# A new issue list for a state-space convolution and a linear attention that share one core

## The chip, the cores and the metric

The kernel runs on one core of one Trainium2 chip. The metric is the device time of one execution in microseconds (us), lower is better. Beside the plain times there is one profiled execution, in which the hardware profiler recorded each instruction of each engine.

## What is computed

Two independent heads read inputs of 2048 rows and 576 columns; their outputs stand side by side in one array of 2048 x 1152.

```python
def _A_ref(u, ...):                     # columns 0..575
    K  = 2.0 * einsum("dn,dnl->dl", C, P).real       # P = exp(A dt * position)
    Kf, Uf = rfft(K, 2 * L), rfft(u transposed, 2 * L)
    y  = irfft(Uf * Kf, 2 * L)[:, :, :L]
    return y transposed + u * D_skip
def _B_ref(x, wqkv, w_phi, wo):         # columns 576..1151, 32 heads of 18
    q, k, v = x @ wqkv
    phi_q, phi_k = softmax of +-(q w_phi), softmax of +-(k w_phi)
    kv, z = phi_k^T v, sum of phi_k
    o = (phi_q kv) / (phi_q z + 1e-6)
    return o @ wo
```

The first head is a long convolution done by Fourier transforms, the second a linear attention with a softmax feature map.

## The kernel before

The program first notes all its work as 2459 numbered operations and then issues them in the order of a written list. An operation is what one engine does in one go: a group of matmuls into one accumulation space (a "PE op"), one vector instruction, one transfer. There is no scheduler at run time: each engine takes its own operations in the order of the list, and an instruction that must wait holds up everything behind it on its engine. SP issues all 345 transfers.

- **Fold and gemms.** The weights are folded with w_phi and split into a high and a low part (wh, wl for the keys, vh, vl for the values). Each of 16 key tiles multiplies 128 rows of x with them (lines 410 to 428; in the rows `wh,x`, `wl,x`, `vh,x`, `vl,x`), splits x itself into two parts (`x<-zo,x`), takes the softmax (lines 430 to 468; its last multiply is `e<-e,small`), copies v, and adds to kv (`e,v`). Each of 16 query tiles does the same for q, transposes (`ident,e` at line 549), multiplies with kv (`kvb,fT`), transposes o (`ident,o`, lines 577 and 578), and multiplies with wo (`wh,x` and `wl,x` again, after the buffers changed hands).
- **Convolution.** 16 first transform stages of u (`ub,w`; the result is copied out of PSUM as `zi` and stored to DRAM), 18 groups that build the filter (`sel,mg` at PE, phases at line 757 on GpSimd, which the profile calls POOL, exponentials on ACT, products at lines 815 to 820 on VectorE, called DVE, and a sum by PE with `cs`), 4 first stages of the filter, 16 products (a turn `ub,ff`, the product itself on DVE and POOL, and a step back `cs,ff`; its factor ff is loaded at line 895, its part ub brought back from DRAM at line 904), and 16 last stages (`zi,w`, four stores each).

Everything that PE makes lies in one PSUM space of 8 banks. A bank can take the next accumulation only when DVE or ACT has copied the last one out (line 300 for a plain copy; lines 310 and 314 are two-operand instructions, of which some read PSUM). The buffers in SBUF turn over too: 2 of ff, zi and mg, 3 of e, ac, x, 5 of ub and cs, 7 of the small sums.

The list is the string ORDER from line 992. A word is an operation's number; an `x` behind it gives the operation to its other engine (DVE and POOL for SBUF work, ACT and DVE for copies out of PSUM), `@` gives the PSUM banks, and `:n` puts n filling matmuls ahead of a PE op. They multiply zeros into the space that the op will overwrite (line 237, rows `ident,zero`), and do nothing for the result; each takes PE's time and stands behind whatever the space has to wait for.

```python
if fill:
    ...
    for _ in range(fill):
        self.matmul(t[0:cols, 0:n], self.zero.t[0:rows, 0:cols], ...)
o[2](eng) if o[12] else o[2]()
...
for word in ORDER.split():
    word, _, fill = word.partition(":")
    word, _, at = word.partition("@")
    k = int(word.rstrip("x"))
    o = self.ops[k]
    ...
    self.emit(k, o, o[12][0] if word[-1] == "x" else o[0], int(fill or 0), at)
```

Before, the list holds 118 filling matmuls at 13 places: 49 at the start of the program, 11 ahead of the third first stage of u, 58 elsewhere.

## Time and profile before

| | |
|---|---|
| median of 3 runs | 544.55 us (543.78 to 545.48) |
| the profiled execution's own time | 545.11 us |
| its span, first to last instruction | 543.3 us |
| mean granted TensorE clock | 0.998 |
| busy: PE, DVE, ACT, POOL | 521.5, 455.9, 382.1, 328.8 us |
| DMA | 107.01 MB, 197 GB/s over the span |

The profile's times start with the span. "Busy" of PE counts matmuls by modelled ends, which overlap a little. A row `psum<-ub,w 64*128 64x288 f32 x8` reads: eight matmuls into PSUM from the weights ub (or w) and the moving tile, in a tile of the array of 64 rows by 128 columns, each on 64 partitions x 288 elements. What stands in brackets is the idle time before the row's first instruction and what ended it. For the reading below the span is cut in three: 0 to 213 us (the key tiles, the first stages of u, the first groups), 213 to 397.6 us (most of the groups, the query tiles' beginning), 397.6 us to the end (products, last stages, the other query tiles).

### The profile page before, as it was taken

Reading aid. Unit: us, or ns where it says so; the run is one execution under the profiler, and the core shown is the slowest. Engines: PE = TensorE matmul, PEld = TensorE weight load, DVE = VectorE, ACT = ScalarE, POOL = GpSimd, SP = SyncE. Lnnn points to the kernel's source line nnn. Section 1 sums busy time; section 2 is a strip of 40 time slices with the busy share of each in tenths; the row PEclk is TensorE's granted clock in tenths of the full one; section 3 lists DMA queues with packets and bytes.
Section 4 is the critical chain, followed back from the end, with each engine's and each line's share of the span. In section 5 each row is a group of like instructions: output and inputs, shape, how many; then the busy total and the mean of one; then the engine's idle time right before and its main releaser. Section 6 shows DMA issues by size and latency. Waiting matters only on the chain.

```text
span 543.3 us, 19242 instructions
## 1 busy us (share of the span) xinstructions
PE 521.5 (96%) x8192; PEld 435.9 (80%) x8192; DVE 455.9 (84%) x716; ACT 382.1 (70%) x555; POOL 328.8 (61%) x456
## 2 busy tenths in 40 slices
PE   8999999999999989999999999999899999999995
PEld 7999899888888767888878666766689877776984
DVE  7999899898868889999989996999974889787641
ACT  4868798798559799889689977989733444343332
POOL 1173885958777775982758998997433617434300
PEclk9999999999999999999999999999999999999999
DMA  8936711244245678246664588756458789998785
GB/s 235 326 105 195 281 45 31 101 139 134 89 139 190 207 241 294 83 128 196 229 205 118 153 265 250 241 180 194 131 173 271 234 281 293 287 281 260 265 252 157
DMA packets 86163, 107.01 MB, mean 197 GB/s; under 512 B 5698, under 2 KB 70338, under 8 KB 86078
## 3 DMA queue, kind: packets, MB, share of 16 engines
q1 hardware_dynamic: 86078, 105.79, 61.5%
q8 instruction: 64, 1.05, 0.8%
q14 instruction: 21, 0.17, 0.1%
HBM read 61.22 MB, written 44.54 MB: 195 GB/s over the span
## 4 chain that ended last, share of the span: by engine, by line
PE 69%; DVE 13%; DMA 7%; ACT 4%; issue 3%; SPq 2%; POOL 1%; DVEq 0%; ACTq 0%; POOLq 0%
PE psum L295 63%; PE psum L549 3%; DMA ff<-in_ff_dram 2%; DMA dram<-zi 2%; PE psum L237 2%; DVE ac L314 1%; DVE cs L816 1%; SPq L979 1%; PE psum L577 1%; DMA cs<-dram 1%; DVE e L310 1%; DMA ub<-dram 1%; DVE e L314 1%; DVE small L434 1%; DVE small L437 1%
## 5 line engine op out<-in xcount | busy, mean ns | idle before, releaser
L295 PE MATMUL psum<-vh,x 128*128 128x288 f32 x576 | 123.6, 301 | 0.5 <-ACT ks L300 0.5
L295 PE MATMUL psum<-wh,x 128*128 128x288 f32 x576 | 124.1, 302 | 0.0
L757 POOL TENSOR_TENSOR cs<-cs,pi 128x32 int32<-128x32 int32 (+4 forms) x180 | 108.5, 608 | 8.0
L295 PEld LDWEIGHTS psum<-wh,x 128*128 128x128 f32 x576 | 94.1, 188 | 7.7 <-issue 4.2
L295 PEld LDWEIGHTS psum<-vh,x 128*128 128x128 f32 x576 | 94.0, 188 | 5.4 <-issue 3.2
L295 PE MATMUL psum<-vl,x 128*128 128x288 f32 x320 | 93.8, 295 | 0.0
L295 PE MATMUL psum<-wl,x 128*128 128x288 f32 x320 | 93.7, 295 | 0.0
L811 ACT ACTIVATE psum<-psum 128x512 f32<-128x512 f32 x108 | 59.9, 588 | 15.4 <-PE psum L295 14.9
L295 PEld LDWEIGHTS psum<-vl,x 128*128 128x128 f32 x320 | 60.2, 188 | 0.0
L295 PEld LDWEIGHTS psum<-wl,x 128*128 128x128 f32 x320 | 60.2, 188 | 0.0
L310 POOL TENSOR_TENSOR x<-zo,x 64x128 fp32r<-64x128 f32 (+1 forms) x30 | 25.4, 848 | 46.3 <-ACT x L394 35.1
L310 POOL TENSOR_TENSOR e<-e,small 128x1152 f32<-128x1152 f32 (+1 forms) x24 | 41.2, 1720 | 14.5 <-DVE small L450 7.8
L815 DVE TENSOR_TENSOR cs<-psum,cs 128x1024 f32<-128x1024 f32 x36 | 43.6, 1212 | 3.7 <-ACT psum L811 3.6
L310 POOL TENSOR_TENSOR e<-small,e 128x576 f32<-128x576 f32 x26 | 30.6, 1177 | 25.4 <-DVE small L437 23.6
L816 DVE TENSOR_TENSOR cs<-psum,cs 128x1024 f32<-128x1024 f32 x36 | 43.6, 1214 | 1.4 <-PE psum L295 1.3
L295 PE MATMUL psum<-ub,ff 64*32 64x288 f32 x1024 | 40.0, 410 | 4.3 <-DMA ff<-in_ff_dram 1.9
L295 PEld LDWEIGHTS psum<-kvb,fT 126*128 126x128 f32 (+1 forms) x320 | 38.3, 188 | 7.2 <-issue 2.9
L295 PEld LDWEIGHTS psum<-cs 128*32 128x32 f32 x2304 | 34.1, 110 | 11.2 <-issue 2.9
L295 PE MATMUL psum<-cs 128*32 128x64 f32 x2304 | 40.0, 220 | 2.6 <-DVE cs L816 0.9
L295 PE MATMUL psum<-kvb,fT 126*128 126x133 f32 (+1 forms) x320 | 41.6, 280 | 0.1
L440 ACT ACTIVATE e<-e 128x1152 f32<-128x1152 f32 x32 | 37.0, 1164 | 2.7 <-POOL e L310 1.3
L781 ACT ACTIVATE cs<-cs 128x1040 f32<-128x1040 int32 x36 | 38.3, 1064 | 0.6 <-POOL cs L776 0.4
(156 smaller groups left out, 1115.2 us busy)
## 6 DMA issues: line engine op xcount, KB each, us to landing
dram<-zi SPq DMA_DIRECT2D x32, 576.0 KB
ub<-dram SPq DMA_DIRECT2D x64, 288.0 KB
dram<-zo SPq DMA_DIRECT2D x32, 288.0 KB
zo<-in_xT_dram SPq DMA_DIRECT2D x24, 320.0 KB
zi<-dram SPq DMA_DIRECT2D x12, 576.0 KB
ub<-in_u_dram SPq DMA_DIRECT2D x16, 288.0 KB
xd<-x SPq DMA_DIRECT2D x8, 576.0 KB
x<-xd SPq DMA_DIRECT2D x8, 576.0 KB
```

Of the source, the lines that this page charges most:

```text
L237: self.matmul(t[0:cols, 0:n], self.zero.t[0:rows, 0:cols], self.data.t[0:rows].bitcast(BF16)[:, 0:n], start=not o[13], stop=not o[13], ski ...
L295: pe.matmul(o, l, r, start=start, stop=stop, skip_group_check=skip)
L310: op(eng, [c_dve(n[0]) if e == "dve" else c_pool(n[1]) for e in eng], lambda e: (dve if e == "dve" else pool).tensor_tensor(dst(), a(), b( ...
L314: op(eng, c_dve(n) if eng == "dve" else c_pool(n), lambda: e.tensor_tensor(dst(), a(), b(), op=alu), r=r, w=w, with_=with_, lock=eng == "p ...
L434: op("dve", c_dve(D), lambda: dve.tensor_reduce(two(top.t), v(), axis=AX.X, op=ALU.max, negate=True), r=[p], w=[top])
L440: op("act", c_act(1152) + 40, lambda: act.activation(e.t, e.t, AF.Exp), r=[e], w=[e], table="exp")
L549: pe.transpose(tp.t[0:m, j - j0, :], e.t[:, sign, 7 * g:7 * g + GRP[g], :].rearrange("p h f -> p (h f)"), ident.t)
L757: op("pool", c_pool(2 * n * W), lambda n=n, j=j: pool.tensor_tensor(x()[:, :, :, n:2 * n], x()[:, :, :, 0:n], pi.t[:, j:j + 2, gs].bitcast ...
L781: act.activation(cs.t[:, 1], cs.t[:, 1].bitcast(I32), AF.Sin, scale=TURN)
L811: op("act", c_act(512), lambda b=b: act.activation(b.t, b.t, AF.Exp), r=[b], w=[b], table="exp")
L815: op("dve", c_dve(64 * W), lambda: dve.tensor_tensor(F(), both(M.t), F(), op=ALU.mult), r=[M, cs], w=[cs])
L816: op("dve", c_dve(64 * W), lambda: dve.tensor_tensor(E.t[:, :, :, 32:64], both(up.t), cs.t[:, :, :, 0:32], op=ALU.mult), r=[up, cs], w=[E])
```

## The change

Only the string ORDER differs: the same 2459 operations with the same tiles, buffers and costs, in another order. The list was made by small moves in which transfers are taken late and delays are random. Its first lines stand for the whole:

```diff
 ORDER = """
-0 1 2 3 1097 1093 4 68 1094 5 1096 1154 1104 1105 1107 1092 1108 1109 51 34 1095 6 27 7@0:49 20 1106 1110 1111 1112 1113 1114 1115 8 35@2 1199 1137 11
-28@4 29 52 12 1116 1120 9 53x 30 36 10 54 13 22@6 32 37 21 1117 39 992 1118 1119 40 15@0 14 1074 23 31 33 1121 38 1063 1003 344 18 25 16 345 24
...
+1093 32 12 22 1116 1154 39 15@0 1117 52 1096 30 38 23 1192 992 344 1094 41 25 1137 14 53 40 54 33 18 31 26 1004@42:2 1118 1076 360 16 24 1119 345 19
+1074 68 346x 1121 17 347 42 1080 1122 1075 1127 287 1123 57@6 56 1161 43 1125 288 348@0 1124 1126 1077 44 1128 1079 1006 1129 1130 349 47 289x 1131 45
...
```

The whole string counts 481 PE ops in both versions. Of the operations, 133 change their engine and 319 their banks; an operation moves by 7 places in the list in the median, by 14 in the mean, and some by hundreds. Filling matmuls: 151 at 43 places in place of 118 at 13; 49 still stand at the start, 2 in place of 11 ahead of the third first stage of u, and 100 in place of 58 elsewhere (2 to 3 at most places).

The first place is on PE, in the first stretch, where the seventh group starts (the trace has it at 188 to 193 us before). `cs` and `e,v` are earlier work, `ub,w` first stages of u, `sel,mg` three parts of the group, `fT,e` transposes of kv. Before:

```order
L295 MATMUL psum<-cs 32x64 x32
L295 MATMUL psum<-e,v_2823 19x36 x32
L295 MATMUL psum<-ub,w_225 128x288 x4
L295 MATMUL psum<-sel,mg 128x512 x2
L295 MATMUL psum<-ub,w_225 128x288 x4
L295 MATMUL psum<-sel,mg 128x512 x2
L295 MATMUL psum<-fT,e 128x126 x5
```

and the changed list, at the same group:

```order
L295 MATMUL psum<-cs 32x64 x32
L295 MATMUL psum<-e,v_2773 19x36 x32
L295 MATMUL psum<-ub,w_219 128x288 x4
L237 LDWEIGHTS zero
L237 MATMUL psum<-ident,zero 128x256
L237 LDWEIGHTS zero
L237 MATMUL psum<-ident,zero 128x256
L295 MATMUL psum<-sel,mg 128x512 x2
L295 MATMUL psum<-ub,w_219 128x288 x4
L237 LDWEIGHTS zero
L237 MATMUL psum<-ident,zero 128x256
```

Two filling matmuls now stand ahead of the group's first part, and four ahead of its second (the first of them is the last row); the neighbours are the same.

The second place is on DVE and POOL, in the key tiles' softmax. `e<-e,small` of 1152 elements is its last multiply, `x<-zo,x` the split of x, `cs<-ac,cs` work of the filter's parameters. Before, on DVE:

```order
L442 TENSOR_REDUCE small<-e 128x2x32 x2
L450 RECIPROCAL small<-small 128x64
L310 TENSOR_TENSOR e<-e,small 128x1152
L310 TENSOR_TENSOR x_552<-zo,x_552 128x512
L310 TENSOR_TENSOR e<-small,e 128x576
L314 TENSOR_TENSOR cs<-ac,cs 128x640
L450 RECIPROCAL small<-small 128x64
L310 TENSOR_TENSOR e<-e,small 128x1152
```

and in the changed list, on POOL (`cs<-cs,pi` is the phases of the filter):

```order
L487 MEMSET v_685 128x32
L752 MEMSET cs 128x16
L310 TENSOR_TENSOR e<-e,small 128x1152
L753 COPY cs<-pi 128x16x2
L757 TENSOR_TENSOR cs<-cs,pi 128x16x2
L757 TENSOR_TENSOR cs<-cs,pi 128x16x2x4
L310 TENSOR_TENSOR x_623<-zo,x_623 64x128
L310 TENSOR_TENSOR e<-e,small 128x1152
```

Of the 16 such multiplies DVE had 4 and POOL 12; now DVE has 1 and POOL 15. Of the 24 splits `x<-zo,x` of 128x512 DVE had 13 and now has 11; POOL does the rest.

The third place is on PE, in the last stretch, at a product's step back (`cs,ff`, which reads the factor ff that a transfer brings). `kvb,fT` is a query tile's product, `ident,o` its transposes. Before:

```order
L295 MATMUL psum<-ub,ff 32x288 x32
L295 MATMUL psum<-kvb,fT 128x133 x8
L295 MATMUL psum<-kvb,fT 128x76 x2
L295 MATMUL psum<-cs,ff 64x288 x16
L577 MATMUL psum<-ident,o 128x128 x4
L578 MATMUL psum<-ident,o 128x128
```

and the changed list:

```order
L295 MATMUL psum<-kvb,fT 128x133 x6
L237 LDWEIGHTS zero
L237 MATMUL psum<-ident,zero 128x256
L237 LDWEIGHTS zero
L237 MATMUL psum<-ident,zero 128x256
L295 MATMUL psum<-kvb,fT 128x133 x2
L295 MATMUL psum<-kvb,fT 128x76 x2
L295 MATMUL psum<-cs,ff 64x288 x16
L237 LDWEIGHTS zero
L237 MATMUL psum<-ident,zero 128x256
L295 MATMUL psum<-vh,x_7078 128x288
```

Here filling matmuls stand inside the query tile's product and behind the step back, and a gemm follows in place of the transposes.

## The prediction

> **What bounds the kernel now.** First the page: the span and the busy shares.

> ```profile
> span 543.3 us, 19242 instructions
> PE 521.5 (96%) x8192; PEld 435.9 (80%) x8192; DVE 455.9 (84%) x716; ACT 382.1 (70%) x555; POOL 328.8 (61%) x456
> ```

> PE is busy for 96% of the span. So a new order can gain at most what PE idles, and it loses whatever it adds to PE's own work. The second view is the table by stretches (columns: stretch, length, busy PE, PEld, DVE, ACT, POOL with counts, granted clock, DMA share, GB/s).

> ```profile
> 0.00:213.00 213.00, 206.42 (x3246) 184.72 (x3246) 185.89 (x283) 168.24 (x226) 137.43 (x220) 1.00 0.52 169
> 213.00:397.60 184.60, 177.93 (x3137) 138.31 (x3137) 174.17 (x273) 158.29 (x236) 141.66 (x197) 1.00 0.59 182
> 397.60:538.30 140.70, 137.12 (x1817) 112.83 (x1809) 95.89 (x163) 54.88 (x92) 49.67 (x40) 1.00 0.83 260
> 538.30:543.30 5.00, 0.00 (x0) 0.00 (x0) 0.00 (x0) 0.65 (x1) 0.00 (x0) 0.82 0.52 171
> ```

> PE idles 213.00 - 206.42 = 6.58 us in the first stretch, 6.67 in the second, 3.58 in the third, and the 5.00 behind its last matmul, where only the last stores run. The clock is 1.00 in all three, so none of this is throttling. DVE is the engine next to the bound: 174.17 of 184.60, 94%, in the middle; DMA is at 0.83 in the last stretch. The third view is PE's list of waits in each stretch (what was waited for, us in total, times, longest): first stretch, middle, last.

> ```profile
> PE psum L295 <- ACT zi L300: 1.7, 2, 1.2
> PE psum L237 <- DVE zero L333: 1.6, 1, 1.6
> PE psum L295 <- DVE zi L300: 0.6, 1, 0.6
> PE psum L295 <- POOL v L487: 0.6, 1, 0.6
> ```

> ```profile
> PE psum L295 <- DMA ub<-dram: 1.5, 2, 1.2
> PE psum L549 <- DVE ac L314: 1.0, 1, 1.0
> PE psum L295 <- DVE cs L816: 0.9, 1, 0.9
> PE psum L295 <- DVE e L314: 0.8, 1, 0.8
> ```

> ```profile
> PE psum L295 <- DMA ff<-in_ff_dram: 1.9, 3, 0.9
> ```

> One wait, 1.6 us for the zeros at the very start, can't be moved by this list. The rest is many small waits, mostly for a PSUM bank that DVE or ACT has yet to copy out, and in the last stretch for the factor ff of a product.

> **The change, part by part.** The sum is made against the profiled execution, 545.11 us (span 543.3 and 1.8 around it), which lies 0.56 above the median of 544.55. Only the order, some engines and the filling matmuls change.

> *Filling matmuls, the sure part.* The timeline of PE around the third first stage of u, and where the eighth group's filler stands before (start, length of the row, line, operation, in brackets the idle time ahead of it; the rows of DVE are the two instructions that hold PE there):

> ```profile
> 14.60 1.26 PE L237 MATMUL psum<-ident,zero 64*128 64x256 bf16 x10
> 15.60 0.51 PE L295 MATMUL psum<-ub,w 64*128 64x288 f32 x1
> ```

> ```profile
> 189.61 1.24 PE L295 MATMUL psum<-ub,w 64*128 64x288 f32 x8 [0.63 <-DVE zi L300]
> 192.03 0.49 PE L295 MATMUL psum<-sel,mg 64*128 64x512 f32 x2 [1.18 <-ACT zi L300]
> ```

> ```profile
> 213.12 0.50 PE L295 MATMUL psum<-sel,mg 64*128 64x512 f32 x2 [0.80 <-DVE e L314]
> 213.79 1.03 PE L237 MATMUL psum<-ident,zero 64*128 64x256 bf16 x8 [0.16 <-DVE zi L300]
> 214.66 1.19 PE L295 MATMUL psum<-ub,w 64*128 64x288 f32 x7
> ```

> Ten fillers from 14.60 to 15.60 are 0.10 us each, and no wait stands at either end: the 9 of 11 that go save 9 x 0.10 = **0.9** (from nothing, if the operands of what follows come late, to 1.0).

> *Filling matmuls, the open part.* 42 more stand elsewhere: 42 x 0.10 = 4.2 us of PE's time. A filler costs nothing where PE would have stood still while it ran. But the rows at 213.79 say that it needn't: it writes the bank that its op will write, waited 0.16 for that bank to be copied out, and then eight of them ran 0.87 (214.66 - 213.79) ahead of the real work. What waits for a bank pays them in full; what waits for an operand (the case of the group's parts, whose selected rows or transposes come late) hides them. The row at 192.03 is the case in which two fillers, 0.2, would be paid or hidden whole: 1.18 of idle time stood there. Bounds 0 and +4.2; I take the middle, **+2.1**, because neither kind is the rule in the waits above.

> *Work moved from DVE to POOL.* The groups of instructions by form (count, busy us and mean ns):

> ```profile
> L310 DVE TENSOR_TENSOR e<-e,small 128x1152 f32<-128x1152 f32 x4 | 5.7, 1426 | 0.1
> L310 DVE TENSOR_TENSOR x<-zo,x 128x512 fp32r<-128x512 f32 x13 | 10.0, 772 | 0.2 <-ACT x L394 0.2
> ```

> ```profile
> L310 POOL TENSOR_TENSOR e<-e,small 128x1152 f32<-128x1152 f32 x12 | 27.3, 2272 | 7.9 <-DVE small L450 7.8
> L310 POOL TENSOR_TENSOR x<-zo,x 128x512 fp32r<-128x512 f32 x11 | 14.2, 1291 | 18.3 <-ACT x L394 18.1
> ```

> Three softmax multiplies and two splits leave DVE: 3 x 1.426 + 2 x 0.772 = 5.8 us less of 185.89 in the first stretch; POOL gains 3 x 2.272 + 2 x 1.291 = 9.4 over 137.43. DVE falls from 87% to 85% there, POOL rises from 65% to 69%, so copies out of PSUM come sooner. The idle time that this and the new order can reach is 6.58 - 1.6 = 5.0. The two waits for `zi` come to 1.7 + 0.6 = 2.3, and the rows at 189.61 and 192.03 put 0.63 and 1.18 of it at the first place shown above, behind copies that a less loaded DVE (and an ACT that takes fewer of them) ends sooner. I take **-2.3**, with 0 and -5.0 as bounds. If POOL is late instead, the cover is gone: see the fourth rival.

> What is left on DVE may get dearer. This row is a split on DVE early in the program, while POOL was hardly at work:

> ```profile
> 11.16 0.69 DVE L310 TENSOR_TENSOR x<-zo,x 128x512 fp32r<-128x512 f32 x1
> ```

> 0.69 against the mean of 0.772 over 13, a tenth more where POOL works beside it. [...]

> *Broken pairs of PE ops.* Counted in the two lists, a gemm follows a gemm directly 4 times less, and a turn `ub,ff` another turn 6 times less. The timeline:

> ```profile
> 448.47 0.30 PE L295 MATMUL psum<-wl,x 128*128 128x288 f32 x1
> 448.61 0.43 PE L295 MATMUL psum<-wh,x 128*128 128x288 f32 x2
> ...
> 450.07 0.29 PE L295 MATMUL psum<-wl,x 128*128 128x288 f32 x1
> 450.29 0.96 PE L295 MATMUL psum<-ub,ff 64*32 64x288 f32 x24
> ```

> ```profile
> 477.33 0.72 PE L295 MATMUL psum<-zi,w 64*32 64x288 f32 x16
> 478.99 2.18 PE L295 MATMUL psum<-ub,ff 64*32 64x288 f32 x64 [0.94 <-DMA ff<-in_ff_dram]
> 481.10 0.40 PE L295 MATMUL psum<-wh,x 128*128 128x288 f32 x1
> 481.34 0.29 PE L295 MATMUL psum<-wl,x 128*128 128x288 f32 x1
> 481.47 0.43 PE L295 MATMUL psum<-wh,x 128*128 128x288 f32 x2
> ```

> Within a gemm the next matmul starts 0.14 later (448.47 to 448.61), into a turn 0.22 (450.07 to 450.29): 0.08 more. Coming back, the first step of a gemm takes 0.24 (481.10 to 481.34) against 0.13 for the next: 0.11 more. So 4 gemms x 0.19 + 6 turns x 0.08 = **+1.2**, between 0.3 and 1.9 (all ten at 0.19). [...]

> *The waits for ff.* Three of them, 1.9 in all, 0.94 at 478.99. Such a transfer lasts longer than the gap it has to fit into, as the chain of what ended last shows (start, length):

> ```profile
> 474.50 4.36 DMA ff<-in_ff_dram
> 486.86 4.95 DMA ff<-in_ff_dram
> ```

> The buffer of ff comes free with an earlier product's step back, and the next transfer runs from there. At the third place shown above and at three more products the changed list puts 0.3 to 0.8 us more of PE's work between the two. I take **-1.2** of the 1.9, bounds 0 and -1.9; late-taken transfers behind other transfers of SP could make it +1.

> *Bank and operand waits in the middle.* The group at 213.12 (0.80 idle) gets its eviction 2.8 us of PE's work earlier, and the 1.0 at line 549 goes in the new neighbourhood: -1.8. Seven PE ops newly stand close behind the copy that they need; I price each with the 0.16 of the row at 213.79, +1.1. Sum **-0.7**, between -2 and +3 (one 0.8 wait at half of the seven), since DVE at 94% in this stretch does no work less.

> The tail behind PE's last matmul, 5.00, has the same operations in nearly the same order: 0.

> Sum: -0.9 + 2.1 - 2.3 + 1.2 - 1.2 - 0.7 = **-1.8**; 545.11 - 1.8 = 543.3 for an execution like the profiled one, 542.75, so **542.8**, on the scale of the median.

> **The rivals.** What can be told apart from no change here is about 0.3%, 1.6 us.

> *The fillers are paid, no wait goes.* The middle stretch keeps its DVE at 94%, banks come as late as now, and fillers behind a bank wait are paid in full as at 213.79. -0.9 + 4.2 + 1.2 = +4.5: 549.1. It decides as soon as more than 13 of the 42 are exposed while all waits stay (13 x 0.10 + 0.3 = 1.6). For it: the row at 213.79. Against it: 5.0 us of idle time lie in a stretch where DVE is relieved.

> *The waits go, and the fillers eat it.* -0.9 - 2.3 + 4.2 + 1.2 - 1.2 - 0.7 = +0.3: 544.9, no change.

> *All goes well.* The first stretch's 5.0 go wholly and the fillers stand only where PE would wait: -0.9 - 5.0 + 0 + 1.2 - 1.2 - 0.7 = -6.6, 538.0. Against it: the waits are many and small, and a list that moves all neighbours seldom takes them all away without new ones.

> *POOL becomes late.* A softmax multiply takes 2.272 on POOL and 1.426 on DVE: the kv product of that key tile gets its operand 0.85 later, behind phases that POOL has queued ahead of it (second place above), and those phases feed the groups. Three such waits are 2.5, and the relief fails: -1.8 + 2.3 + 2.5 = +3.0, 547.6. Against it: with twelve such multiplies on POOL the first stretch shows one wait for POOL, 0.6.

> **How the numbers follow.** The forecast gets 0.40, and its own range is 540.5 to 545.0: 0.30 of it lie more than 1.6 us below the median, 0.10 within. The second rival (544.9) gets 0.15, the third (538.0) 0.12, the first (549.1) 0.18, the fourth (547.6) 0.15. Faster by over 0.3%: 0.30 + 0.12 = 0.42; within: 0.10 + 0.15 = 0.25; slower: 0.18 + 0.15 = 0.33. For the range I leave out what lies below the third rival and above the first by more than half of one of the smaller terms: 538.0 to 549.5.

> **What would show it.** In the profile of the changed kernel: the row of fillers ahead of the third first stage of u has 2 in place of 10, and the stages behind it come 0.9 sooner; the rows `ident,zero` elsewhere carry bracketed idle time, or stand where none would be (paid); PE's idle time in the first stretch falls from 6.6 towards 4.3, with DVE's busy time there about 180; the group at 213 has no wait for DVE's `e`; the waits for ff come to about 0.7. PE's busy time should be 1 to 4 us more. Wrong would be: first-stretch idle time as before or waits on POOL's `e` (the fourth rival), or busy time up by over 4 with idle time as before (the first).

## The result

The changed kernel is slower: 550.57 us in the median of 4 runs (549.37 to 551.48) against 544.16 of the kernel before (542.90 to 545.48), a ratio of 1.0116 with a 95% interval of 1.0084 to 1.0148. In a second measurement, on the chip of the run after_again below, it was 1.0155 (1.0129 to 1.0181). Forecast were 542.8, with a range from 538.0 to 549.5.

The page of the changed kernel, the span and the busy times:

```profile
span 548.7 us, 19305 instructions
PE 525.4 (96%) x8225; PEld 439.6 (80%) x8225; DVE 453.8 (83%) x711; ACT 374.3 (68%) x550; POOL 344.0 (63%) x465
```

The table by stretches, with the last two borders moved by the 5.4 us that the span is longer (columns as in the prediction):

```profile
0.00:213.00 213.00, 205.98 (x3255) 186.09 (x3255) 179.26 (x277) 164.07 (x225) 150.92 (x227) 0.99 0.53 172
213.00:397.60 184.60, 177.16 (x3053) 137.29 (x3051) 172.96 (x267) 155.62 (x233) 140.44 (x197) 0.99 0.57 180
397.60:543.70 146.10, 141.68 (x1922) 115.93 (x1920) 101.62 (x169) 53.95 (x92) 52.60 (x41) 0.99 0.79 248
```

PE is busy for 3.9 us more and idle for 1.5 more. The granted clock, in the column behind the counts, is 0.99 in each stretch, where it was 1.00. And PE's waits have other names. The lists below are cut a little later, at 220 and 403 us, to hold the same work: first stretch, middle, last.

```profile
PE psum L295 <- DVE wl L367: 2.3, 1, 2.3
PE psum L295 <- issue: 1.9, 3, 1.0
...
PE psum L237 <- ACT zi L300: 1.2, 1, 1.2
PE psum L295 <- ACT zi L300: 0.5, 2, 0.3
```

```profile
PE psum L237 <- DVE ac L314: 1.0, 2, 0.9
PE psum L295 <- DVE cs L815: 1.0, 2, 0.6
PE psum L577 <- ACT zo L608: 0.9, 1, 0.9
```

```profile
PE psum L295 <- DMA cs<-dram: 2.0, 1, 2.0
PE psum L577 <- DVE o L314: 1.1, 1, 1.1
PE psum L295 <- ACT zo L300: 0.4, 1, 0.4
PE psum L295 <- DMA ff<-in_ff_dram: 0.4, 1, 0.4
```

Some old waits shrank as forecast (ff 1.9 to 0.4, the parts of a group behind `zi` from 1.18 to 0.3 at most), and others came, two of them about 2 us long, longer than any that the kernel before had behind its start. (`issue` is idle time for which the profile shows no releaser; it was 0.3 in the first stretch before.)

To see where the time goes, one can compare how far both are with the same work. I gave each PE op its usual price, summed the prices in the order of each list, and compared the times at which the sums reach the same value. (The prices are the 20th percentile of the intervals of that kind of op in both traces. Another choice of prices moves single entries by up to about 1 us; the last entry is read from the two traces alone.)

```
time before     20.2  61.9  144.2  198.5  209.2  234.4  287.2  376.8  423.0  529.9  last matmul
changed - before -1.6  -2.6   -2.4   -2.9   +0.2   +1.2   +0.7   +2.3   +3.6   +2.6   +6.5
```

So the first 198 us win 2.9, the next 36 lose 4.1, the 295 us behind that lose 1.4, and the last 8 us lose 3.9. Behind the last matmul 4.5 us of stores follow, 5.6 before.

The largest loss has one place. PE around it (start, length, idle time in brackets):

```profile
199.89 0.29 PE L295 MATMUL psum<-wl,x 128*128 128x288 f32 x1
202.45 2.29 PE L295 MATMUL psum<-ub,w 64*128 64x288 f32 x8 [2.26 <-DVE wl L367]
204.67 0.61 PE L295 MATMUL psum<-wh,x 128*128 128x288 f32 x1
205.07 0.44 PE L295 MATMUL psum<-wl,x 128*128 128x288 f32 x1
...
205.84 0.43 PE L295 MATMUL psum<-wh,x 128*128 128x288 f32 x2
```

and the same place microsecond by microsecond, in the columns of the table by stretches:

```profile
201.00:202.00 1.00, 0.00 (x0) 0.00 (x0) 0.36 (x3) 1.00 (x4) 1.00 (x2) 1.00 0.98 390
202.00:203.00 1.00, 0.55 (x2) 0.50 (x4) 0.50 (x3) 1.00 (x2) 1.00 (x1) 0.58 1.05 429
203.00:204.00 1.00, 1.00 (x6) 0.68 (x4) 0.00 (x0) 1.00 (x2) 0.31 (x2) 0.50 0.95 389
204.00:205.00 1.00, 1.00 (x5) 0.34 (x2) 0.22 (x1) 1.00 (x2) 1.00 (x1) 0.50 0.92 207
205.00:206.00 1.00, 1.00 (x7) 1.00 (x7) 1.00 (x2) 1.00 (x2) 0.94 (x1) 0.71 0.97 343
```

PE stands still for 2.26 us, and just as it goes on, its clock is granted at 0.50, for 3.41 us (202.17 to 205.58). The first stage of u, 1.24 long elsewhere, takes 2.29. The trace has two more such stretches of 3.41 us before the last matmul, at 215.82 and at 536.67, each behind waits (1.23 and 2.02). They count as busy PE: that is where part of the 3.9 us comes from.

### The profile page after: what moved, and what is told of

The parts are those of the page before. It is cut to its first block, busy times and chain, and to the rows that moved or that the text cites. A ratio compares the mean times of both kernels' runs of the same rounds, so it can differ in the third digit from the quotient of the medians.

```text
span 548.7 us, 19305 instructions
## 1 busy us (share of the span) xinstructions
PE 525.4 (96%) x8225; PEld 439.6 (80%) x8225; DVE 453.8 (83%) x711; ACT 374.3 (68%) x550; POOL 344.0 (63%) x465
## 4 chain that ended last, share of the span: by engine, by line
PE 70%; DVE 11%; ACT 8%; issue 4%; DMA 3%; POOL 3%; SPq 0%; DVEq 0%; ACTq 0%; POOLq 0%
PE psum L295 64%; PE psum L549 2%; PE psum L237 2%; DVE ac L314 1%; ACT psum L811 1%; DMA cs<-dram 1%; PE psum L577 1%; DVE cs L815 1%; POOL e L310 1%; ACT cs L785 1%; DVE cs L816 1%; DMA x<-xd 1%; DMA ff<-in_ff_dram 1%; ACT L811 1%; ACT zi L300 1%
## 5 line engine op out<-in xcount | busy, mean ns | idle before, releaser
L295 PE MATMUL psum<-vh,x 128*128 128x288 f32 x576 | 125.0, 304 | 0.3 <-DVE e L314 0.2
L295 PE MATMUL psum<-wh,x 128*128 128x288 f32 x576 | 124.1, 302 | 0.8 <-issue 0.6
L757 POOL TENSOR_TENSOR cs<-cs,pi 128x512 int32<-128x512 int32 (+4 forms) x180 | 107.1, 607 | 5.4
L295 PEld LDWEIGHTS psum<-wh,x 128*128 128x128 f32 x576 | 94.6, 189 | 8.2 <-issue 4.6
L295 PEld LDWEIGHTS psum<-vh,x 128*128 128x128 f32 x576 | 95.4, 191 | 6.6 <-issue 3.7
L295 PE MATMUL psum<-vl,x 128*128 128x288 f32 x320 | 94.5, 297 | 0.0
L295 PE MATMUL psum<-wl,x 128*128 128x288 f32 x320 | 93.9, 295 | 0.0
L310 POOL TENSOR_TENSOR e<-e,small 128x1152 f32<-128x1152 f32 (+1 forms) x30 | 50.5, 1688 | 21.1 <-DVE small L314 14.9
L295 PEld LDWEIGHTS psum<-vl,x 128*128 128x128 f32 x320 | 61.0, 191 | 0.0
L295 PEld LDWEIGHTS psum<-wl,x 128*128 128x128 f32 x320 | 60.6, 189 | 0.0
L310 POOL TENSOR_TENSOR x<-zo,x 64x128 fp32r<-64x128 f32 (+1 forms) x29 | 25.7, 885 | 35.7 <-ACT x L394 26.6
L310 POOL TENSOR_TENSOR e<-small,e 128x576 f32<-128x576 f32 x26 | 31.0, 1195 | 22.9 <-DVE small L437 21.3
L816 DVE TENSOR_TENSOR cs<-psum,cs 128x1024 f32<-128x1024 f32 x36 | 43.7, 1214 | 0.4 <-PE psum L295 0.2
L295 PE MATMUL psum<-ub,ff 64*32 64x288 f32 x1024 | 41.5, 410 | 1.7 <-ACT zo L300 0.4
L295 PEld LDWEIGHTS psum<-kvb,fT 126*128 126x128 f32 (+1 forms) x320 | 38.4, 189 | 5.2 <-issue 0.9
L295 PE MATMUL psum<-kvb,fT 126*128 126x133 f32 (+1 forms) x320 | 41.2, 278 | 0.4 <-DVE cs L815 0.4
L295 PE MATMUL psum<-cs 128*32 128x64 f32 x2304 | 40.6, 221 | 0.8 <-DVE cs L820 0.6
L295 PEld LDWEIGHTS psum<-cs 128*32 128x32 f32 x2304 | 34.9, 110 | 8.0 <-issue 3.4
```

The lines of the kernel that those rows point to most:

```text
L295: pe.matmul(o, l, r, start=start, stop=stop, skip_group_check=skip)
L310: op(eng, [c_dve(n[0]) if e == "dve" else c_pool(n[1]) for e in eng], lambda e: (dve if e == "dve" else pool).tensor_tensor(dst(), a(), b( ...
L757: op("pool", c_pool(2 * n * W), lambda n=n, j=j: pool.tensor_tensor(x()[:, :, :, n:2 * n], x()[:, :, :, 0:n], pi.t[:, j:j + 2, gs].bitcast ...
L816: op("dve", c_dve(64 * W), lambda: dve.tensor_tensor(E.t[:, :, :, 32:64], both(up.t), cs.t[:, :, :, 0:32], op=ALU.mult), r=[up, cs], w=[E])
```

## The experiments

The first reading was that of a late load (theory L). The load for the first stage at 202.45 is issued at 194.50 in the changed list and 129.69 in the old one, and `wl` at line 367 seemed done long before. The wait of 2.0 for cs near the end has a load as late. Rivals: fillers are the cost (F), the stall alone counts and the clock does not follow it (W), SP's stores set the end (S). Four kernels were run on one chip. All ratios below are to the kernel before, run beside them on the same chip; the changed kernel itself gave 1.0116 in one such measurement and 1.0155 in another, so ratios from two such measurements compare only to about 0.004, 2 us.

```diff
 changed list: load of u, first stage 0
-... 1034@26 387 394 ... 415 993 ...
+... 1034@26 993 387 394 ... 415 ...
```

> The changed list, with one word moved: the load of u for first stage 0 is issued some 11 us sooner, before two weight loads. Theory L (late loads and the clock): in the changed kernel this load is issued at 194.50 and PE, ready for it at 200.19, starts at 202.45; 2.3 us of standing still, and from 202.16 to 205.57 the granted clock is 0.50, which costs about 1.2 more. So the wait at 200 goes, the clock there stays at 1.00, and the time falls by 2.5 to 4, to a ratio of 1.004 to 1.007 to the kernel before. Rival F (the 42 added filling matmuls are what was paid): the wait is used up by the next bank wait, time falls by under 1, ratio 1.010 or more. Rival W (the stall alone counts, the clock does not follow it): -2.0 at most, and the clock is low somewhere else.

```diff
 changed list: load of cs, last stage 11
-... 2410 2457 2458 ... 2424 2437 ...
+... 2410 2424 2457 2458 ... 2437 ...
```

> The changed list, with one word moved: the load of cs for last stage 11 is issued behind that of last stage 9, some 6 us sooner, ahead of eight output stores. Theory L: in the changed kernel PE waits 2.02 for it at 534.2, and the granted clock is 0.50 from 536.7 to 540.0, about 1.4 more; so time falls by 2 to 3.5, ratio 1.005 to 1.008. Rival S (SP's issue of stores at about 0.63 each sets the end, not PE): PE ends sooner but the time falls by under 1, ratio 1.010 or more, since the stores behind the load are as many as before. Rival F: under 1 as well.

Both moves together:

> The changed list with both words moved. Theory L: the two add up, -5 to -7 us, the ratio to the kernel before is 0.998 to 1.003 and nothing else of the change costs much on balance. Rival F: -1 to -3, ratio 1.006 to 1.010. Rival S: as the first of the two alone, -3, ratio 1.005.

```diff
 changed list: fillers ahead of the two PE ops
-... 994@24 ... 2425@2 ...
+... 994@24:20 ... 2425@2:18 ...
```

> The changed list with both loads as late as they are, and filling matmuls ahead of the two PE ops that wait for them: 20 ahead of first stage 0 of u and 18 ahead of last stage 11. They need a free bank, not the load, so by theory L they run while PE would stand still: waits as long as before, but PE looks busy, the clock stays at 1.00 behind them, and the time falls by 1.5 to 2.6, ratio 1.006 to 1.010. If low clock has nothing to do with the stall (rival W): no change or +0.5 to +1, ratio 1.011 to 1.014, with the clock low at the same places.

Measured, in this order: 1.0124 (1.0090 to 1.0159), 1.0134 (1.0098 to 1.0171), 1.0150 (1.0116 to 1.0183) and 1.0227 (1.0188 to 1.0265). Theory L fell. With the load 11 us sooner, PE of u0_early waits as before:

```profile
203.64 1.47 PE L295 MATMUL psum<-ub,w 64*128 64x288 f32 x8 [2.27 <-DVE wl L367]
```

In fill_cover the fillers themselves waited 2.26 for `wl`, since it is the bank that isn't free, and then ran in front of the real work; the clock fell all the same: over the first 213 us it is 0.98 in the mean, 0.99 in the other three. The 38 cost 4 to 5 us against the other three (557.80 against 552.37 to 553.79). That is the danger that the prediction saw in the row at 213.79. In l11_early PE's wait for cs is gone, and its last matmul comes at 543.9 where u0_early's comes at 544.5; yet the two spans, 550.6 and 550.5, are the same. SP issues 20 stores in a row there, with two more behind them before the end:

```profile
532.93 13.38 SPq L979 DMA_DIRECT2D out_dram<-ot  x20
```

That is 0.67 each, and the row ends at 546.3, behind the last matmul. So for the end rival S fits: this wait of PE was not on the path alone. (Rival F forecast the same time; the row of stores speaks for S.) The trace of both_early shows the link. There the wait for cs is gone too, and PE waits as long at the next gemm, for a copy by ACT that itself waits for a store to free its buffer:

```profile
535.10 0.40 PE L295 MATMUL psum<-vh,x 128*128 128x288 f32 x1 [2.03 <-ACT ot L300]
534.40 0.65 ACT L300 ACTIVATE ot<-psum 128x576 f32<-128x576 f32 x1 [6.60 <-DMA out_dram<-ot]
```

The name in the bracket at 202.45 was right, then, and one has to follow it. DVE and ACT of the changed kernel ahead of 202:

```profile
198.24 0.28 DVE L300 COPY e<-psum 36x133 f32<-36x133 f32 x1
201.64 0.25 DVE L300 COPY e<-psum 36x95 f32<-36x95 f32 x1 [3.12 <-ACT e L300]
201.81 0.58 DVE L367 TENSOR_TENSOR wl<-psum,wh 128x72 fp32r<-128x72 f32 x2
```

```profile
196.06 1.28 ACT L781 ACT_TABLE_LOAD   x1
197.35 1.07 ACT L781 ACTIVATE cs<-cs 128x1040 f32<-128x1040 int32 x1
198.33 1.15 ACT L785 ACTIVATE cs<-cs,hp 128x1040 f32<-128x1040 f32 x1
199.38 1.06 ACT L781 ACTIVATE cs<-cs 128x1040 f32<-128x1040 int32 x1
200.34 1.15 ACT L785 ACTIVATE cs<-cs,hp 128x1040 f32<-128x1040 f32 x1
201.39 0.38 ACT L300 ACTIVATE e<-psum 36x76 f32<-36x76 f32 x2
```

Two short copies into the buffer e stand on ACT behind a table load and four waves, 5.3 us of work. A DVE copy into the same buffer waits 3.12 for the first of them. Behind it on DVE stand the two small `wl` instructions, and only they free the bank of the first stage of u (theory Q). The remedy is two letters:

```diff
 changed list: two kv copies, ACT to DVE
-... 374 ... 369 ...
+... 374x ... 369x ...
```

The next four ran on one chip. head_new and tail_old are sewn from both lists: the first words of one, then all operations not yet issued in the order of the other.

> The changed kernel once more, unchanged, as the base for the other runs on this chip. All theories: 1.008 to 1.016 against the kernel before.

> The changed list with two words given to the other engine: two copies of the kv sums out of PSUM (76 columns of 36 rows each) go from ACT to DVE. In the changed kernel they stand on ACT behind a table load and four waves; a DVE copy into the same buffer waits 3.12 for the first of them at 201.64, with the two wl instructions behind it that free the bank of first stage 0 of u. Theory Q (a queue on a queue: PE's wait at 200 is this DVE wait, which is this ACT queue; the low clock follows the wait): the wait of 2.3 goes, so does the 3.4 us of half clock behind it, and the time falls by 2.5 to 4, 0.005 to 0.007 below the run of the changed kernel beside it. Rival F (the added filling matmuls are the cost): under 1 us, ratio within 0.002 of it.

> A list sewn of both: the first 806 words of the changed list (to about 185 us), then all other operations in the order and with the banks, engines and fillers of the list before. In the traces PE of the changed kernel is 2.5 to 2.9 us ahead at 170 to 198 us (the same base work done) and 6.5 behind at its last matmul. Theory Q, and with it that the loss lies behind this point: faster than the kernel before by 1 to 3 us, ratio 0.994 to 0.998. Rival F, or a cost that the changed list's first part hands on (buffers, POOL late): 1.000 to 1.006.

> A list sewn of both: the first 2339 words of the changed list (to about 510 us), then the rest as in the list before. At that place PE of the changed kernel is 2.5 us behind, at the end 6.5; behind its last matmul come 4.5 us of stores, 5.6 in the kernel before. Theory T (the last stretch of the list costs some 2 to 4 by itself, by the late load of cs with its half clock and by SP's stores): 0.004 to 0.007 below the changed kernel beside it, at about 1.005 to the kernel before. Rival: the tail only hands on what comes late, the ratio stays within 0.002 of the changed kernel's.

Measured: after_again 1.0155 (1.0129 to 1.0181), copies_dve 1.0071 (1.0041 to 1.0100), head_new 0.9937 (0.9921 to 0.9952), tail_old 1.0148 (1.0129 to 1.0166). Theory Q held: the two letters take 0.0084, 4.6 us, and the intervals don't meet. PE of copies_dve at this place:

```profile
200.45 0.29 PE L295 MATMUL psum<-wl,x 128*128 128x288 f32 x1
200.67 1.24 PE L295 MATMUL psum<-ub,w 64*128 64x288 f32 x8
201.84 0.40 PE L295 MATMUL psum<-wh,x 128*128 128x288 f32 x1
...
202.60 0.43 PE L295 MATMUL psum<-wh,x 128*128 128x288 f32 x2
```

No wait, and no half clock before its last matmul. From the first stage's start to the fourth row it takes 1.93 here (200.67 to 202.60) and 3.39 in the changed kernel (202.45 to 205.84): 1.5 us is what the half clock cost there, beside 2.26 of waiting. The rest lies near the second stretch at half clock, which copies_dve, at 0.999 over its span, doesn't have; in its place it has a wait of 1.02 for DVE's `e` at 223. Over the whole span PE is busy for 4.3 us less, with as many instructions and fillers:

```profile
PE 521.1 (96%) x8225; PEld 436.7 (80%) x8225; DVE 454.2 (83%) x713; ACT 373.6 (69%) x548; POOL 344.5 (63%) x465
```

So three stretches at half clock come to 4.3 us, an estimated 1.4 each.

head_new shows the other side: the changed list's first 806 words, to about 185 us, are a gain that lasts, 0.0063 or 3.4 us. This sewn list beats both kernels (541.33 us against 545.00). Theory T fell with tail_old: with the old list's last 120 words the loss is the same, and PE still waits for cs:

```profile
PE psum L295 <- DMA cs<-dram: 1.4, 1, 1.4
```

Left over are the fillers and the second half. The four kernels of the next chip:

```diff
 copies_nofill: copies_dve without its fillers behind the third first stage of u
-... 1482@72:2 ... 2057@4:3 ...
+... 1482@72 ... 2057@4 ...
 second_new: the first 1304 words of the list before, then the changed list
 second_nofill: second_new without the 63 fillers behind the seam
 before_u2: the list before
-... 1004@42:11 ...
+... 1004@42:2 ...
```

> The changed list with the two kv copies on DVE, and without its 100 filling matmuls beside the 49 at the start and the 2 at the third first stage of u. With them, that list took 1.0071 of the kernel before. Theory F (fillers are paid, 0.10 us each): up to 10 us less, ratio 0.990 to 0.997. Theory H (they stand mostly where PE would wait for the same thing anyway): 0 to 4 us less, 1.000 to 1.007, with PE's idle time up by what the fillers took. Theory K (they keep the clock up): more stretches of half clock than the none of that run, and no gain.

> A list sewn the other way: the first 1304 words of the list before (to about 284 us), then the rest in the changed order with its banks, engines and its 63 fillers there (the list before has 43 there). In the trace of the list with the two copies on DVE, PE is 3.0 us ahead at 287 us and 1.5 behind at its last matmul. Theory M (the middle and end of the changed list lose 4 to 5 us by themselves): ratio 1.007 to 1.010. Rival: that loss was handed on from the first half (buffers and transfers that came another way): 0.999 to 1.004.

> The same sewn list without the 63 fillers behind the seam. Theory F: 63 x 0.10 = 6.3 us less than the run beside it, 0.010 to 0.012 lower in ratio. Theory H: 0 to 2.5 less, 0 to 0.005 lower, with more idle time of PE. Theory K: equal or higher, with stretches of half clock that the other run has not.

> The kernel before with one number changed: 2 fillers in place of 11 ahead of the third first stage of u. By the prediction's term 9 x 0.10 = 0.9 us less, ratio 0.998, and the same wait list. Rival (the next operands come late, or the waits behind take it back): 0.9995 to 1.001, with a wait near 16 us.

Measured: 1.0077 (1.0052 to 1.0103), 1.0128 (1.0100 to 1.0156), 1.0141 (1.0106 to 1.0177), 1.0043 (1.0022 to 1.0064). Theory F, which forecast 6.3 to 10 us less, is out. Without its 100 fillers copies_dve is no faster (1.0077 for 1.0071, on two chips), without its 63 second_new is no faster (1.0141 for 1.0128, on one chip). PE is busy for 514.3 us in copies_nofill, 6.8 less, and the time isn't:

```profile
PE 514.3 (94%) x8125; PEld 428.7 (79%) x8125; DVE 453.2 (83%) x713; ACT 373.7 (68%) x548; POOL 344.0 (63%) x465
```

Both lists without fillers have a lower clock in their profiles, as theory K had it: 0.992 in copies_nofill against 0.999 in copies_dve, 0.993 in second_nofill against 0.999 in second_new. Every execution's record bears it out: the mean granted clock is 0.984 to 0.993 in the 12 runs of copies_nofill against 0.990 to 0.999 in the 11 of copies_dve, and 0.981 to 0.993 in second_nofill against 0.992 to 0.999 in second_new. In the mean 0.007 is missing, an estimated 7 us more at half clock in each execution (some of it behind the last matmul, where it costs nothing): about two stretches, an estimated 2 to 3 us. How much the waits cost that the fillers had covered isn't separated from it. before_u2 shows the same on a small scale: nine fillers fewer, and the list isn't faster but slower by 2.3 us. In its trace the first stage now waits for its own load:

```profile
15.40 1.24 PE L295 MATMUL psum<-ub,w 64*128 64x288 f32 x8 [0.24 <-DMA ub<-in_u_dram]
```

and a wait of 1.6 for POOL's phases appears later in the same stretch. Its profiled execution has the span of the kernel before, 543.3; where others of its 12 runs (544.78 to 549.53) lost over 4 us more isn't seen in it.

second_new puts the larger part of the loss, 7 us, into the second half by itself. What it loses is idle time of PE:

```profile
PE 522.3 (95%) x8212; PEld 436.7 (79%) x8212; DVE 462.3 (84%) x719; ACT 380.8 (69%) x553; POOL 326.6 (59%) x455
```

Its profiled span is 549.7, so PE is idle for 27.4 us, 5.6 more than before, and busy for only 0.8 more; its clock is 0.999. Fillers, broken pairs and half clock are not what it loses by in this execution. Three more runs cut the second half in two, and took two of its waits away:

```diff
 mid_new: 1304 words before, changed to about 454 us, then before
 last_new: 2081 words before (to about 450 us), then changed
 turns_later: copies_dve with two query turns behind the next PE op
-... 619@23 577@4 ... 724@67 ... 737 ...
+... 577@4 619@23 ... 737 724@67 ...
```

> Three pieces: the first 1304 words of the list before (to about 284 us), then the changed list to about 454 us, then what is left as in the list before. The sewn list with all of the changed second half took 1.0128. Theory M1 (the loss lies in the query tiles and groups between 284 and 454: copies by ACT and DVE that come 0.4 to 1.1 late at a dozen places): 1.007 to 1.012. Theory T1 (it lies in the last 90 us: the late cs and the stores behind each other): 1.000 to 1.004.

> The list before to its word 2081 (about 450 us), then the changed list. Theory M1: 1.000 to 1.004. Theory T1: 1.007 to 1.012. If the two runs' losses add up to clearly less than 0.0128, the pieces hand lateness to each other.

> The changed list with the two copies on DVE (1.0071), and two turns of query tiles moved behind the next PE op: that which waits 1.08 for DVE's o at 421 us behind a 2.0 us gemm, that which waits 0.88 for ACT's division at 313 behind one of 0.4. Theory M1: each wait was the order's own, 1.0 to 1.5 us less, ratio 1.004 to 1.005, if PE's lead is kept to the end. Theory S (SP's stores set the end): waits gone, the time the same within 0.001.

Measured: 1.0074 (1.0045 to 1.0102), 1.0081 (1.0051 to 1.0112), 1.0049 (1.0026 to 1.0071). Neither theory has it alone: the two halves of the second half cost 4 us each, and together (0.0155) about what they cost in one (0.0128). The waits are many small ones, in mid_new from 284 to 452 us

```profile
PE psum L295 <- ACT fT L300: 1.1, 1, 1.1
PE psum L577 <- DVE o L314: 1.1, 1, 1.1
PE psum L237 <- DVE ac L314: 1.0, 2, 0.8
PE psum L577 <- ACT zo L608: 0.9, 1, 0.9
```

and in last_new behind 452:

```profile
PE psum L295 <- DMA cs<-dram: 2.2, 1, 2.2
PE psum L295 <- DMA zi<-dram: 1.9, 2, 1.5
```

In mid_new's profile PE is idle for 4.0 us more than before (546.8 less 521.0 busy). In last_new's it is idle for 0.8 more and busy for 2.9 more (547.0 less 524.4), with a mean clock of 0.995 in place of 0.998.

By the comparison of equal work turns_later loses nothing at 413 to 423 us, where copies_dve loses 1.1, so that wait was the order's own. The other move failed: the wait of 0.88 near 313 is gone, and the transposes that now come first wait 1.16 for DVE's `cs`, to 316.75. The ratio is 0.0022 lower than copies_dve's, as theory M1 had it, but on another chip and with intervals that meet: likely, not shown.

## Why the prediction was wrong

The direction was wrong. The first 198 us went as forecast; the waits behind them did not.

- **First stretch** (-0.9 fillers, -2.3 waits): right in sum to 198 us, and not to the stretch's own border at 213. PE is 2.9 ahead at 198 us, and head_new keeps 3.4. But the idle time of the stretch, which was to fall from 6.6 towards 4.3, is 7.02: the waits for `zi` shrank from 2.3 to 0.9 (one of 1.23 stands just behind the border), and the new wait of 2.26 at 200 us took their place. The share of the nine fillers can't be had alone; taken out of the old list by themselves (before_u2) they made it slower.
- **Work moved to POOL**: DVE's busy time in the first stretch is 179.26, as forecast, and what was left on DVE didn't get dearer (a split takes 0.767 in the mean, 0.772 before). POOL was not "hardly at work" beside the split at 11.16, but busy for 0.57 of its 0.69. Of the 13 splits of the kernel before, the six with POOL idle take 0.68 to 0.69 each; of the seven beside POOL's work, three take 0.69 to 0.70 and four 0.95 to 0.98.
- **42 other fillers** (+2.1): mis-sized, as far as the runs can tell. Taking all 100 away gave 1.0077 for 1.0071, so on balance they cost about 0, within some 2 us. The first rival came near the time (549.1) by a mechanism that the runs refute.
- **Broken pairs of PE ops** (+1.2): no run takes this term by itself; it stays open. No run shows the 0.3 at its lower end either: the rows give 0.08 to 0.19 for a pair, 0.8 to 1.9 for all ten.
- **The waits for ff** (-1.2): right, 1.9 went to 0.4.
- **The waits, in the first stretch and in "Bank and operand waits in the middle ... Sum -0.7"**: this is the step that failed. It followed the old waits to their end, gave no new wait to the first stretch and seven of 0.16 each to the middle. The changed list has new waits of 2.26 at 200 us, inside the first stretch, and of 1.23 at 214, and about ten of 0.4 to 1.1 behind them; copies_dve takes 4.6 us off at the first place, second_new puts 7 us behind 284. The new waits don't follow from how many instructions stand between a copy and its user, which I had counted, but from what stands ahead of the copy on its own engine: a short copy behind 5.3 us of ACT work, a DVE queue behind that copy, PE behind that queue. And of the two old waits that were to go, 1.8 in all, the one of 1.0 for DVE's `ac` only changed its name; the fillers now stand behind it:

```profile
358.55 0.38 PE L237 MATMUL psum<-ident,zero 128*126 128x256 bf16 x2 [0.86 <-DVE ac L314]
```

- **"The clock is 1.00 in all three, so none of this is throttling"**: true of the one profiled execution, and read as if it held for any list (other executions of the kernel before have 0.990 to 0.999 in the mean). In the changed kernel's profile half clock came with the waits of 2.26 and 2.02, and cost 1.5 us at the one place where it could be measured by itself. The sum had no term for it.
- **The tail** (0): behind PE's last matmul came 5.6 us, not the 5.00 of the prediction, whose window began 0.6 later; now it is 4.5. Ahead of it, PE's wait for cs rose from 0.4 to 2.0, but that load's place was not what cost (l11_early); where the wait was taken away in both_early, one as long for a buffer held by the stores came instead. What makes the stores late stays open: PE, late there, waits for cs in all of tail_old (1.4), mid_new (1.2) and last_new (2.2), and head_new, whose PE is 3 us early there, has no wait above 0.3 behind 505 us.
- **POOL late** (fourth rival): fell in the first stretch; POOL has 150.92 there in place of 137.43 and no wait for it stands in PE's list.

## What to carry to other kernels

In a list written out by hand or by a search, a short instruction is as late as everything ahead of it on its engine (here two copies of 0.38 behind 5.3 us on ACT); check for each bank and buffer that PE needs what its last user stands behind, and behind whom that one stands, over all queues. A releaser in a trace that looks long done is followed back before another is put in its place: here the name was right, and the load looked at first was innocent. To find which part of a reordered list wins and which loses, sew the two lists at a place where buffers and banks agree: head_new came out of it, faster than both.

## What the runs showed of the hardware

```profile
202.17:205.58 3.41, 3.13 (x12) 2.10 (x13) 1.12 (x4) 3.41 (x5) 2.72 (x2) 0.50 0.99 341
215.82:219.23 3.41, 3.41 (x41) 2.30 (x42) 3.02 (x4) 2.47 (x5) 2.73 (x3) 0.50 0.02 6
536.67:540.08 3.41, 3.41 (x26) 3.06 (x14) 0.80 (x2) 0.92 (x2) 0.00 (x0) 0.50 0.48 119
```

They begin 0.28 us before the end of the wait of 2.26 (202.45), 1.17 behind the end of the wait of 1.23 (214.65) and 0.44 behind the end of that of 2.02 (536.23). A wait of 2.15 to 2.30 us stands near 200 us in seven profiles (the changed kernel's, u0_early, l11_early, both_early, fill_cover, tail_old, after_again), and each of them is slower behind it: in six a single matmul `wl,x`, 0.29 to 0.30 long ahead of the wait, takes up to 0.44 or 0.45 within the 5 us behind it, and in fill_cover the clock over the first 213 us is 0.98. In copies_dve, where that wait is gone, the clock from 199 to 204 us is 1.00 and `wl,x` stays at 0.29 to 0.30. The wait of 1.23, for ACT's `zi`, is in other profiles too: u0_early, both_early and fill_cover have it (1.2) at a clock of 1.00 over 213 to 397.6 us, and copies_dve (1.2) and second_new, with a wait of 1.7 for cs behind 505 us, have 0.999 over the whole span. From what length on a wait brings half clock along isn't shown. The two profiled executions of the changed list have a mean clock of 0.989 and 0.990. Over its ten executions it runs from 0.987 to 0.996, so part of its scatter probably comes from there.

Priced as these traces show it, a new wait of 2.26 us costs its length and 1.5 us more, and the forecast had neither.
